# Padded heads of rounded k, single q buffers and a 24th resident weight tile in an attention and soft mixture-of-experts kernel

## The chip, the cores and the metric

The kernel runs on one core of a Trainium2 chip. It is one launch: causal attention over 96 heads, then a soft mixture of experts on the result. The metric is the device time of the launch in microseconds; smaller is better. Engine names are those of the profile: PE (TensorE, matmul), PEld (its weight loads), DVE (VectorE), ACT (ScalarE), POOL (GpSimd), SP (SyncE, which issues most DMAs).

## The reference

```python
# attention: batch 8, heads 12, seq 448, head_dim 64
scores = q @ k.T / 8, causal mask, softmax over keys      # per head
attn = softmax(scores) @ v
x = attn, transposed to (8 * 448, 768)
# soft mixture of experts: 8 experts of 4 slots, hidden 1024
logits = x @ phi                                          # (3584, 32)
d = softmax(logits, over tokens); c = softmax(logits, over slots)
slot_input = (d.T @ x) by expert                          # 8 x 4 x 768
slot_out = relu(slot_input @ w1[e]) @ w2[e]
out = c @ slot_out                                        # (3584, 768)
```

All is float32. q and k are drawn eight times larger than is usual, so the scores need the full precision.

## The kernel before

**Pairs and blocks.** Two heads make a pair; there are 48 pairs and 96 heads, head i = 2p + h. The function `block(p)` runs once per pair and works on several pairs at once: it finishes the scores of pair p, begins those of pair p + 1, prepares the operands of pairs p + 1 to p + 3, and multiplies the probabilities of pair p with v. Every engine executes its instructions in the order in which the program issues them (`_InOrder`); engines wait for each other through semaphores. So the text of `block` is the order of each queue.

**Scores in two passes.** The float32 matmul is replaced by matmuls with operands rounded to fp32r. The first pass (`scores1`) multiplies `ks` by `qd`. Rows 0 to 63 of `ks` hold the rounded k, rows 64 to 127 the remainder of k; `qd` holds the rounded q twice. The second pass (`scores2`) adds `k2` times `r2`: rows 64 to 127 are rounded k and the remainder of q, and the first rows carry the negative row maximum, block by block of 32 queries. In between, DVE reduces the first-pass scores to the maximum of each block of 32 queries (`max_keys`, `max_row`) and POOL spreads it into the first 14 rows of `r2` (`max_spread`, an affine_select). After the second pass ACT takes the exponential (`exps`).

**Preparing a pair.** The operands of a pair q come from HBM as raw q and raw k (`load_qk`). ACT rounds them (`cast_k` into `ks`, `cast_q` into `qd`), POOL computes the remainders in place (`sub_k` into rows 64 to 127 of `ks`, `sub_q` into rows 64 to 127 of `r2`), and ACT copies rounded k into `k2` (`copy_k2`). `ks`, `qd` and `r2` have two buffers, taken in turn by pairs; `k2` has one. The raw tiles rotate through a pool of four, so that a load waits for the subtraction that read the tile before.

**The order inside a block** (before), by engine, for a middle block p with heads a = 2p and a + 1:

- PE: second pass of head a, first pass of a + 2, second pass of a + 1, first pass of a + 3, probabilities times v for the pair, row maxima, parts of the experts' logits, four transposes.
- POOL: `sub_q(p+1)`, `sub_k(p+2)`, spread for head a + 2, spread for head a + 3. In block 4 it also clears `si`, the slot sums.
- ACT: exponential of head a, a copy of transposed x, exponential of a + 1, `copy_k2(p+1)`, `cast_q(p+2)`, `cast_k(p+3)`, and a few small operations of the logits in some blocks (`m6` = p modulo 6 tells which).
- SP: v of pair p + 1, in odd blocks one tile of expert weights, raw q of p + 3 (waits for `sub_q(p+1)`), raw k of p + 4 (waits for `sub_k(p+2)`).

```python
        if p:
            sub_q(p + 1)
            load_qk(p + 3, 0)
            sub_k(p + 2)
            load_qk(p + 4, 1)
        ...
        copy_k2(p + 1)
        ...
        cast_q(p + 2)
        cast_k(p + 3)
```

**Expert weights.** They are 64 tiles of 768 KB. `RES` = 23 tiles have places of their own from the start (eleven double tiles in `wres` and one single in `wone`) and are loaded in the odd blocks of attention. `TW1` = 12 more lie in a pool that opens when the buffers of attention are given back; each of its tiles lies over certain attention buffers and its load waits until those are free. SP issues them in order. All later tiles reuse places of tiles that the experts have consumed, so that their loads wait for PE. After them come the output's DMAs, 11 MB.

**The start.** Before block 0 the operands of pairs 0 and 1 are prepared by halves (one head at a time), and some matmuls on constants (`warm`, with counts in `START`) keep PE busy. Memsets on DVE and POOL clear padding and constants.

Of the kernel before, what the change touches and what calls it, by code (L numbers as in the profile page):

```python
# [9 lines left out]
F32 = mybir.dt.float32  # L10
# [3 lines left out]
ALU = mybir.AluOpType  # L14
# [18 lines left out]
NR, XB, XT = 2, 3, 2  # L33
RES, TW1 = 23, 12

HT = 2
WN, PAD = 1536, 168
WARM = (2, 5, 2, 3, 3)
START = (8, 3, 2)

# [40 lines left out]
def attention_soft_moe(ctx: ExitStack, tc: tile.TileContext, qk, va, phi, w1, w2, out):  # L81
    nc = _Core(tc)
    const = ctx.enter_context(tc.tile_pool(name="const", bufs=1, side="left"))
    wone = ctx.enter_context(tc.tile_pool(name="wone", bufs=1, side="left"))
    wres = ctx.enter_context(tc.tile_pool(name="wres", bufs=RES // 2, side="left"))
# [5 lines left out]
    fix = early.enter_context(tc.tile_pool(name="fix", bufs=1, side="right"))  # L91
    raw = early.enter_context(tc.tile_pool(name="raw", bufs=4, side="right"))
    ps_1 = att.enter_context(tc.tile_pool(name="ps_1", bufs=1, space=PSUM))
# [5 lines left out]
    x_, va_, pt_ = [None] * XB, [None, None], [None, None]  # L99
    qd_, ks_ = [fix.tile([P, 2, S], F32R, name="qd0")], [fix.tile([P, 2 * S + KP], F32R, name="ks0")]  # L100
    r2_ = [fix.tile([P, 2, S], F32R, name="r20")]
    qd_.append(fix.tile([P, 2, S], F32R, name="qd1"))
    ks_.append(fix.tile([P, 2 * S + KP], F32R, name="ks1"))
    va_[0] = fix.tile([P, NCH, 2, VC], F32, name="va0")
    x_[1] = fix.tile([P, NCH, 3 * P], F32, name="x1")
    r_ = [fix.tile([P, RW], F32, name=f"r{i}") for i in range(2)]
    k2_ = fix.tile([P, 2 * S + KP], F32R, name="k2")
    r2_.append(fix.tile([P, 2, S], F32R, name="r21"))
    pt_[0] = wk.tile([P, 1024], F32, name="pt0")
    va_[1] = wk.tile([P, NCH, 2, VC], F32, name="va1")  # L110
    pt_[1] = wk.tile([P, 1024], F32, name="pt1")
    ltn = moe.tile([P, P + 1], F32, name="lt")
    lt = ltn[:, 0:P]

    x_[2] = moe.tile([P, NCH, 3 * P], F32, name="x2")
    x_[0] = moe.tile([P, NCH, 3 * P], F32, name="x0")
    gs = moe.tile([P, P], F32, name="gs")
    mk = moe.tile([P, P], F32, name="mk")

    st = {}  # L120

    def load_qk(p, a, hs=slice(0, 2), eng=nc.sync):
        if p < NPAIR:
            if hs.start == 0:

                st["raw", a, p] = (wres.tile([P, 2 * WN], F32, tag="w", name=f"qk{a}_{p}")[:, 0:2 * S]
                                   .rearrange("p (h s) -> p h s", h=2)
                                   if (p, a) in ((1, 0), (2, 1)) else
                                   raw.tile([P, 2, S], F32, tag="qk", name=f"qk{a}_{p}"))
            eng.dma_start(out=st["raw", a, p][:, hs], in_=qk[p, :, a, hs])  # L130
# [20 lines left out]
    def slot(n, name, dtype=F32):  # L151
        m = place(n)
        if m >= RES:
            return wt[0].tile([P, WN], dtype, tag=f"wa{m}", name=name)
        if m == RES - 1:
            return wone.tile([P, WN], dtype, tag="w1", name=name)
        k = (n - m, m // 2)
        if k not in twos:
            twos[k] = wres.tile([P, 2 * WN], F32, tag="w", name=name)
        t = twos[k][:, WN * (m % 2):WN * (m % 2) + WN]  # L160
        return t if dtype is F32 else t.bitcast(dtype)

    def load_w(n):
        if n < len(order):
            m, e, h, u = order[n]
            t = wtiles[order[n]] = slot(n, f"w{n}")
            src, q = (w1 if m == 0 else w2)[e, h], place(n)
            if n <= NBUF or q >= RES - 1:
                nc.sync.dma_start(out=t, in_=src[:, WN * u:WN * u + WN])
            elif u:  # L170

                nc.sync.dma_start(out=twos[n - q, q // 2], in_=src)

    for hs in (slice(0, 1), slice(1, 2)):
# [20 lines left out]
    po0 = po2[:, 0:NCH]  # L195
    identb = const.tile([P, P], BF16, name="identb")

    for x in (x_[1], x_[0], x_[2]):
        nc.vector.memset(x[:, NCH - 1], 0.0)
    nc.scalar.activation(out=identb, in_=ident, func=AF.Copy)  # L200
    load_qk(1, 1, eng=nc.scalar)
    load_qk(2, 0)
    load_qk(3, 1)
    for i in range(NR):
        nc.gpsimd.memset(r2_[i][0:64, :, :].bitcast(F32), 0.0)
        nc.vector.memset(ks_[i][:, 2 * S:2 * S + KP].bitcast(F32), 0.0)
        nc.vector.memset(r_[i], -3.0e38)
    nc.vector.memset(k2_[0:64, 0:2 * S].bitcast(F32), 1.0)
    nc.vector.memset(k2_[:, 2 * S:2 * S + KP].bitcast(F32), 0.0)

# [12 lines left out]
    def kv(p):  # L223
        return ks_[p % NR][:, 0:2 * S].rearrange("p (h s)->p h s", h=2)

    def cast_q(p, hs=slice(0, 2)):
        if p < NPAIR:
            nc.scalar.activation(out=qd_[p % NR][:, hs], in_=st["raw", 0, p][:, hs], func=AF.Copy)

# [9 lines left out]
    def copy_k2(p, hs=slice(0, 2)):  # L239
        if p < NPAIR:  # L240
            nc.scalar.activation(out=k2_[64:P, 0:2 * S].rearrange("p (h s)->p h s", h=2)[:, hs], in_=kv(p)[0:64, hs],
                                 func=AF.Copy)

    def sub_q(p, hs=slice(0, 2), eng=None):
        if p < NPAIR:
            (eng or nc.gpsimd).tensor_tensor(out=r2_[p % NR][64:P, hs], in0=st["raw", 0, p][64:P, hs],
                                             in1=qd_[p % NR][64:P, hs], op=ALU.subtract)


    def scores1(i, part):  # L250
        if i >= NHD:
            return
        p, h = divmod(i, 2)
        ks, qd = ks_[p % NR], qd_[p % NR]
        if ("s", i) not in st:
# [7 lines left out]
        if part[0] == "k":  # L263
            c = int(part[1])
            o, w, m = S * h + P * c, S - CQ0[c], min(P, S - P * c + (KP if i > 4 or i % 2 else 0))
            nc.tensor.matmul(s[0:m, SCOL[c]:SCOL[c] + w], ks[:, o:o + m],
                             qd[:, h, CQ0[c]:S], start=start, stop=False, skip_group_check=True)
            return
# [46 lines left out]
    def max_spread(i):  # L315
        if i >= NHD:
            return
        p, h = divmod(i, 2)
        mr = st.pop(("mr", i))

        nc.gpsimd.affine_select(out=r2_[p % NR][0:NQB, h].rearrange("p (b t)->p b t", t=32),
                                in_=mr.unsqueeze(1).to_broadcast([NQB, NQB, 32]),
                                compare_op=ALU.is_equal, fill=0.0, base=0,
                                pattern=[[-1, NQB], [0, 32]], channel_multiplier=1)

    def scores2(i, cs):
        if i >= NHD:
            return
        p, h = divmod(i, 2)
        s = st["s", i]  # L330
        k2, r2 = k2_, r2_[p % NR]
        for c in cs:
            o, w, m = S * h + P * c, S - CQ0[c], min(P, S - P * c + (KP if i > 4 or i % 2 else 0))
            nc.tensor.matmul(s[0:m, SCOL[c]:SCOL[c] + w], k2[:, o:o + m],
                             r2[:, h, CQ0[c]:S], start=False, stop=True, skip_group_check=True)
# [152 lines left out]
    run_z = const.tile([P, 1], F32, name="run_z")  # L488
    si = const.tile([P, DM], F32, tag="si", name="si")
    lg = const.tile([P, NB, NCH, NSLOT], F32, name="lg")  # L490
# [477 lines left out]
```

## Time and profile before

| | |
|---|---|
| median of three runs | 404.35 us (403.54 to 404.68) |
| the profiled execution | 403.89 us, span 402.2 us |
| granted TensorE clock, mean | 0.984 |
| busy: PE, DVE, ACT, POOL | 368.3, 293.7, 282.4, 265.3 us |
| DMA moved | 119.17 MB, mean 296 GB/s |

The span is the time from the first to the last instruction. All instructions carry the same source line (a helper's, L65), so the rows are told apart by engine, operation and tiles. In a timeline row the columns are the start, the duration, engine, line, operation, written tile and read tiles, shapes and count; in brackets stands the idle time of the engine before it and what ended it. On PE, `s<-qd,ks` is the first pass and `s<-r,k` the second. On POOL, `r<-qk,qd` is `sub_q`, `ks<-qk,ks` is `sub_k`, and the affine select `r<-mr` is a spread. On ACT, `qd<-qk` is `cast_q`, `ks<-qk` is `cast_k`, `k<-ks` is `copy_k2`, `pt<-s` the exponential. On SP, `w<-in_w_dram` are expert weights. The name `r` stands for `r2`, for the maxima and for a few more, since numbers are left out of names.

### The profile page before, as it was taken

How to read it: one execution, taken by the hardware profiler on the slowest of the kernel's cores; microseconds unless marked ns; L12 is line 12 of the kernel's file. 1: busy time of each engine (PE TensorE's matmuls, PEld its weight loads, DVE VectorE, ACT ScalarE, POOL GpSimd, SP SyncE). 2: the span in 40 equal slices, each digit the busy share in tenths (PEclk: the TensorE clock that was granted, in tenths of full speed). 3: DMA queues.
4: the chain of work that ended last, by engine and by line, in shares of the span. 5: the costliest groups of instructions: out<-in, count | busy, mean ns of one | idle time of the engine just before them, and what ended most of it. 6: DMA issues, size and time to landing. Idle time of an engine off the chain costs nothing.

```text
span 402.2 us, 14066 instructions
## 1 busy us (share of the span) xinstructions
PE 368.3 (92%) x5756; PEld 295.8 (74%) x5756; DVE 293.7 (73%) x834; ACT 282.4 (70%) x395; POOL 265.3 (66%) x214
## 2 busy tenths in 40 slices
PE   6889899999999999999999999999999989997840
PEld 3678888898988898888888889888876544542420
DVE  5868788788898888898888888888975575342540
ACT  5878798898898888888888988988952112432430
POOL 5899899898898988898988989888950000000000
PEclk9999999999999999999999999999999999999985
DMA  8668877878787788777788787788679999999997
GB/s 304 230 199 282 271 266 228 245 279 278 229 286 262 244 269 289 256 240 265 262 270 259 249 272 238 274 286 257 216 279 415 420 420 423 424 418 413 398 397 339
DMA packets 34480, 119.17 MB, mean 296 GB/s; under 512 B 3824, under 2 KB 8944, under 8 KB 32880
## 3 DMA queue, kind: packets, MB, share of 16 engines
q1 hardware_dynamic: 34128, 117.55, 82.2%
q8 instruction: 45, 0.74, 0.7%
q10 hardware_dynamic: 288, 0.73, 0.5%
q14 instruction: 19, 0.16, 0.1%
HBM read 107.25 MB, written 11.01 MB: 294 GB/s over the span
## 4 chain that ended last, share of the span: by engine, by line
PE 54%; DMA 16%; POOL 12%; issue 5%; ACT 4%; DVE 4%; SPq 1%; POOLq 0%; DVEq 0%; ACTq 0%
PE s L65 28%; PE po L65 17%; DMA w<-in_w_dram 14%; POOL r L65 7%; POOL ks L65 5%; PE xm L65 3%; PE rt L65 1%; ACT ks L65 1%; PE pp L65 1%; DVE r L65 1%; DMA qk<-in_qk_dram 1%; PE hp L65 1%; ACT k L65 1%; DVE si L65 1%; PE e L65 1%
## 5 line engine op out<-in xcount | busy, mean ns | idle before, releaser
L65 DVE TRANSPOSE_TENSOR_REDUCE r<-s 128x32 f32<-128x1024 f32 x96 | 119.5, 1245 | 11.4 <-PE s L65 9.3
L65 ACT ACTIVATE pt<-s 128x1024 f32<-128x1024 f32 x96 | 98.8, 1029 | 40.6 <-PE s L65 37.8
L65 PEld LDWEIGHTS po<-va,pt 128*64 128x64 f32 x3040 | 103.6, 138 | 12.0 <-issue 11.9
L65 PE MATMUL po<-va,pt 128*64 128x65 f32 x3040 | 110.6, 224 | 0.0
L65 POOL TENSOR_TENSOR r<-qk,qd 64x896 fp32r<-64x896 f32 (+1 forms) x50 | 101.7, 2033 | 5.5 <-ACT qd L65 1.8
L65 POOL TENSOR_TENSOR ks<-qk,ks 64x896 fp32r<-64x896 f32 (+1 forms) x49 | 99.2, 2024 | 0.2
L65 PE MATMUL s<-qd,ks 128*128 128x448 f32 (+4 forms) x384 | 80.8, 322 | 0.6 <-POOL ks L65 0.4
L65 POOL TENSOR_SCALAR_AFFINE_SELECT r<-mr 14x448 fp32r<-14x448 f32 x96 | 61.5, 643 | 29.8 <-PE xm L65 18.6
L65 PE MATMUL s<-r,k 128*128 128x448 f32 (+3 forms) x384 | 65.2, 292 | 5.0 <-POOL r L65 4.3
L65 PEld LDWEIGHTS s<-r,k 128*128 128x128 f32 (+1 forms) x384 | 59.3, 176 | 11.0 <-POOL r L65 8.8
L65 PEld LDWEIGHTS s<-qd,ks 128*128 128x128 f32 (+2 forms) x384 | 52.8, 184 | 3.7 <-issue 1.4
L65 ACT ACTIVATE qd<-qk 128x896 fp32r<-128x896 f32 (+1 forms) x50 | 46.0, 920 | 1.7 <-DMA qk<-in_qk_dram 0.8
L65 ACT ACTIVATE k<-ks 64x896 fp32r<-64x896 f32 (+1 forms) x49 | 45.8, 934 | 1.2
L65 ACT ACTIVATE ks<-qk 128x896 fp32r<-128x896 f32 (+1 forms) x51 | 45.4, 892 | 1.1 <-DMA qk<-in_qk_dram 1.0
L65 PE MATMUL s<-tri,identb 128*128 128x192 bf16 x192 | 39.4, 270 | 1.1 <-DVE si L65 0.4
L65 DVE TENSOR_REDUCE r<-r 128x16 f32<-128x32 f32 x192 | 33.7, 176 | 5.0
L65 DVE TENSOR_REDUCE mr<-s 14x32 f32<-14x128 f32 x47 | 13.1, 279 | 23.1 <-ACT ks L65 12.8
L65 PE MATMUL xm<-ident,x 128*128 128x128 f32 x188 | 28.3, 273 | 0.0
L65 ACT ACTIVATE xts<-xm 128x512 f32<-128x512 f32 x47 | 27.8, 592 | 0.2 <-PE xm L65 0.2
L65 DVE TENSOR_SCALAR x<-po,sm 64x64 f32<-64x64 f32 x94 | 25.9, 276 | 0.7
L65 DVE TENSOR_TENSOR x<-po,sm 128x384 f32<-128x384 f32 (+2 forms) x49 | 25.7, 526 | 0.0
L65 DVE COPY ot<-pp 128x384 f32<-128x384 f32 x26 | 13.6, 554 | 13.4 <-PE pp L65 13.3
(138 smaller groups left out, 391.0 us busy)
## 6 DMA issues: line engine op xcount, KB each, us to landing
qk<-in_qk_dram SPq DMA_DIRECT2D x93, 448.0 KB, 4.4
w<-in_w_dram SPq DMA_DIRECT2D x43, 768.0 KB, 7.0
w<-in_w_dram SPq DMA_DIRECT2D x10, 1536.0 KB, 21.0
va<-in_va_dram SPq DMA_DIRECT2D x47, 260.0 KB, 4.6
out_dram<-ot SPq DMA_DIRECT2D x16, 384.0 KB, 6.7
out_dram<-ot SPq DMA_DIRECT2D x2, 1536.0 KB, 9.2
qk<-in_qk_dram SPq DMA_DIRECT2D x4, 224.0 KB, 3.9
hw<-in_w_dram SPq DMA_DIRECT2D x1, 768.0 KB, 8.4
```

Source lines behind the costliest of these rows:

```text
L65: return self._tc.keep_in_program_order(op(*args, **kwargs))
```

## The change

- Two zero columns stand behind each head of `ks` and `k2` (row of 2 x 450 instead of 2 x 448 + 2), so that the last chunk of either head reads zeros and not its neighbour. Operations on k now address two runs of 448.
- `qd` and `r2` have one buffer each. In a middle block POOL does `sub_k(p+2)` first, then `sub_q(p+1)`; ACT does `cast_k(p+3)` first, then `cast_q(p+2)`; the loads follow. Blocks 0 and 1 have an order of their own by halves.
- The raw tiles are two fixed ones for k and two for q, and the order of buffers in memory changes.
- `RES` = 24 and `TW1` = 11: twelve double tiles are resident, `wone` is gone, and blocks 16 and 30 load a weight tile as well as the odd blocks up to 43.
- `si` is cleared by DVE before all pairs and no longer by POOL in block 4.
- At the start, k of pair 1 is loaded through SP's queue and no longer through ACT's; the warm-up counts change from (8, 3, 2) to (9, 6, 2, 4).

```diff
+KS = S + KP
-RES, TW1 = 23, 12
+RES, TW1 = 24, 11
-START = (8, 3, 2)
+START = (9, 6, 2, 4)
...
-    wone = ctx.enter_context(tc.tile_pool(name="wone", bufs=1, side="left"))
-    raw = early.enter_context(tc.tile_pool(name="raw", bufs=4, side="right"))
...
+    kraw = {n: fix.tile([P, 2, S], F32, name=f"kraw{n}") for n in (0, 1)}
+    qraw = {0: fix.tile([P, 2, S], F32, name="qraw0")}
+    ks_ = [fix.tile([P, 2 * KS], F32R, name="ks0")]
+    qd = fix.tile([P, 2, S], F32R, name="qd")
+    ks_.append(fix.tile([P, 2 * KS], F32R, name="ks1"))
+    qraw[1] = fix.tile([P, 2, S], F32, name="qraw1")
     va_[0] = fix.tile([P, NCH, 2, VC], F32, name="va0")
+    r_ = [fix.tile([P, RW], F32, name=f"r{i}") for i in range(2)]
     x_[1] = fix.tile([P, NCH, 3 * P], F32, name="x1")
-    k2_ = fix.tile([P, 2 * S + KP], F32R, name="k2")
-    r2_.append(fix.tile([P, 2, S], F32R, name="r21"))
+    k2_ = fix.tile([P, 2 * KS], F32R, name="k2")
+    r2 = fix.tile([P, 2, S], F32R, name="r2")
...
     for hs in (slice(0, 1), slice(1, 2)):
         load_qk(0, 1, hs)
         load_qk(0, 0, hs)
+    load_qk(1, 1)
     load_qk(1, 0)
...
-    load_qk(1, 1, eng=nc.scalar)
     load_qk(2, 0)
-    load_qk(3, 1)
...
+    nc.vector.memset(si, 0.0)
...
-            o, w, m = S * h + P * c, S - CQ0[c], min(P, S - P * c + (KP if i > 4 or i % 2 else 0))
+            o, w, m = KS * h + P * c, S - CQ0[c], min(P, KS - P * c)
...
     sub_k(0, h1)
+    load_qk(3, 1)
     max_row(0, 0)
...
-        if p % 2 and p // 2 < RES - 1 or p == 2 * RES - 2:
-            load_w(p // 2)
+        if p % 2 and p < 44 or p in (16, 30):
+            load_w(st["w"])
+            st["w"] += 1
...
         if p == 0:
             copy_k2(0, h1)
             cast_q(1, h1)
+            warm(START[3], pob)
             max_row(1, 0)
...
-        elif p == 4:
-            nc.gpsimd.memset(si, 0.0)
...
-        if p:
+        late_k = p == 1
+        if p == 1:
+            sub_q(2, h0)
+            sub_k(3, h0)
+            sub_q(2, h1)
+            load_qk(4, 0)
+        elif p:
+            sub_k(p + 2, h0 if late_k else slice(0, 2))
+            if not late_k:
+                load_qk(p + 4, 1)
             sub_q(p + 1)
             load_qk(p + 3, 0)
-            sub_k(p + 2)
-            load_qk(p + 4, 1)
         else:
             sub_q(1, h0)
+            sub_q(1, h1)
+            load_qk(3, 0)
             sub_k(2, h0)
         copy_k2(p + 1)
...
-        cast_q(p + 2)
-        cast_k(p + 3)
+        if p:
+            cast_k(p + 3)
+            cast_q(p + 2)
+        else:
+            cast_q(2)
+            cast_k(3)
...
         max_spread(a + 2)
         if p == 0:
-            sub_q(1, h1)
-            load_qk(3, 0)
+            sub_k(2, h1)
+            load_qk(4, 1)
...
         max_spread(a + 3)
-        if p == 0:
-            sub_k(2, h1)
-            load_qk(4, 1)
+        if late_k:
+            sub_k(p + 2, h1)
+            load_qk(p + 4, 1)
```

More of the change, by code (lines that the diff above doesn't have):

```diff
@@ L99, in attention_soft_moe, with heads @@
     x_, va_, pt_ = [None] * XB, [None, None], [None, None]
[L100 to L103, printed above, removed]
+    kraw = {n: fix.tile([P, 2, S], F32, name=f"kraw{n}") for n in (0, 1)}
[4 more added lines that the diff above has]
+    qraw[1] = fix.tile([P, 2, S], F32, name="qraw1")
     va_[0] = fix.tile([P, NCH, 2, VC], F32, name="va0")
+    r_ = [fix.tile([P, RW], F32, name=f"r{i}") for i in range(2)]
     x_[1] = fix.tile([P, NCH, 3 * P], F32, name="x1")
-    r_ = [fix.tile([P, RW], F32, name=f"r{i}") for i in range(2)]
-    k2_ = fix.tile([P, 2 * S + KP], F32R, name="k2")
-    r2_.append(fix.tile([P, 2, S], F32R, name="r21"))
+    k2_ = fix.tile([P, 2 * KS], F32R, name="k2")
+    r2 = fix.tile([P, 2, S], F32R, name="r2")
     pt_[0] = wk.tile([P, 1024], F32, name="pt0")
+    pt_[1] = wk.tile([P, 1024], F32, name="pt1")
     va_[1] = wk.tile([P, NCH, 2, VC], F32, name="va1")
-    pt_[1] = wk.tile([P, 1024], F32, name="pt1")
+    x_[2] = moe.tile([P, NCH, 3 * P], F32, name="x2")
+    x_[0] = moe.tile([P, NCH, 3 * P], F32, name="x0")
     ltn = moe.tile([P, P + 1], F32, name="lt")
     lt = ltn[:, 0:P]
-    x_[2] = moe.tile([P, NCH, 3 * P], F32, name="x2")
-    x_[0] = moe.tile([P, NCH, 3 * P], F32, name="x0")
     gs = moe.tile([P, P], F32, name="gs")
     mk = moe.tile([P, P], F32, name="mk")
-    st = {}
+    st = {"w": 0}
+    def heads(t):
+        return t.rearrange("p (h s) -> p h s", h=2)
     def load_qk(p, a, hs=slice(0, 2), eng=nc.sync):
@@ L128, in load_qk @@
                                    if (p, a) in ((1, 0), (2, 1)) else
-                                   raw.tile([P, 2, S], F32, tag="qk", name=f"qk{a}_{p}"))
+                                   kraw[p % 2 if p > 1 else 1 - p] if a else qraw[p % 2 if p else 1])
             eng.dma_start(out=st["raw", a, p][:, hs], in_=qk[p, :, a, hs])
@@ L154, in slot @@
             return wt[0].tile([P, WN], dtype, tag=f"wa{m}", name=name)
-        if m == RES - 1:
-            return wone.tile([P, WN], dtype, tag="w1", name=name)
         k = (n - m, m // 2)
@@ L167, in load_w @@
             src, q = (w1 if m == 0 else w2)[e, h], place(n)
-            if n <= NBUF or q >= RES - 1:
+            if n <= NBUF or q >= RES:
                 nc.sync.dma_start(out=t, in_=src[:, WN * u:WN * u + WN])
@@ L196, in attention_soft_moe @@
     identb = const.tile([P, P], BF16, name="identb")
+    si = const.tile([P, DM], F32, tag="si", name="si")
     for x in (x_[1], x_[0], x_[2]):
@@ L200, in attention_soft_moe @@
     nc.scalar.activation(out=identb, in_=ident, func=AF.Copy)
-    load_qk(1, 1, eng=nc.scalar)
     load_qk(2, 0)
-    load_qk(3, 1)
+    nc.gpsimd.memset(r2[0:64, :, :].bitcast(F32), 0.0)
     for i in range(NR):
-        nc.gpsimd.memset(r2_[i][0:64, :, :].bitcast(F32), 0.0)
-        nc.vector.memset(ks_[i][:, 2 * S:2 * S + KP].bitcast(F32), 0.0)
+        nc.vector.memset(heads(ks_[i])[:, :, S:KS].bitcast(F32), 0.0)
         nc.vector.memset(r_[i], -3.0e38)
-    nc.vector.memset(k2_[0:64, 0:2 * S].bitcast(F32), 1.0)
-    nc.vector.memset(k2_[:, 2 * S:2 * S + KP].bitcast(F32), 0.0)
+    nc.vector.memset(k2_[0:64, :].bitcast(F32), 1.0)
+    nc.vector.memset(heads(k2_)[:, :, S:KS].bitcast(F32), 0.0)
+    nc.vector.memset(si, 0.0)
     def misc(name):
@@ L223, in kv @@
     def kv(p):
-        return ks_[p % NR][:, 0:2 * S].rearrange("p (h s)->p h s", h=2)
+        return heads(ks_[p % NR])[:, :, 0:S]
     def cast_q(p, hs=slice(0, 2)):
         if p < NPAIR:
-            nc.scalar.activation(out=qd_[p % NR][:, hs], in_=st["raw", 0, p][:, hs], func=AF.Copy)
+            nc.scalar.activation(out=qd[:, hs], in_=st["raw", 0, p][:, hs], func=AF.Copy)
     def cast_k(p, hs=slice(0, 2)):
@@ L240, in copy_k2 @@
         if p < NPAIR:
-            nc.scalar.activation(out=k2_[64:P, 0:2 * S].rearrange("p (h s)->p h s", h=2)[:, hs], in_=kv(p)[0:64, hs],
+            nc.scalar.activation(out=heads(k2_)[64:P, hs, 0:S], in_=kv(p)[0:64, hs],
                                  func=AF.Copy)
@@ L245, in sub_q @@
         if p < NPAIR:
-            (eng or nc.gpsimd).tensor_tensor(out=r2_[p % NR][64:P, hs], in0=st["raw", 0, p][64:P, hs],
-                                             in1=qd_[p % NR][64:P, hs], op=ALU.subtract)
+            (eng or nc.gpsimd).tensor_tensor(out=r2[64:P, hs], in0=st["raw", 0, p][64:P, hs],
+                                             in1=qd[64:P, hs], op=ALU.subtract)
     def scores1(i, part):
@@ L253, in scores1 @@
         p, h = divmod(i, 2)
-        ks, qd = ks_[p % NR], qd_[p % NR]
+        ks = ks_[p % NR]
         if ("s", i) not in st:
@@ L319, in max_spread @@
         mr = st.pop(("mr", i))
-        nc.gpsimd.affine_select(out=r2_[p % NR][0:NQB, h].rearrange("p (b t)->p b t", t=32),
+        nc.gpsimd.affine_select(out=r2[0:NQB, h].rearrange("p (b t)->p b t", t=32),
                                 in_=mr.unsqueeze(1).to_broadcast([NQB, NQB, 32]),
@@ L330, in scores2 @@
         s = st["s", i]
-        k2, r2 = k2_, r2_[p % NR]
+        k2 = k2_
         for c in cs:
-            o, w, m = S * h + P * c, S - CQ0[c], min(P, S - P * c + (KP if i > 4 or i % 2 else 0))
+            o, w, m = KS * h + P * c, S - CQ0[c], min(P, KS - P * c)
             nc.tensor.matmul(s[0:m, SCOL[c]:SCOL[c] + w], k2[:, o:o + m],
@@ L488, in attention_soft_moe @@
     run_z = const.tile([P, 1], F32, name="run_z")
-    si = const.tile([P, DM], F32, tag="si", name="si")
     lg = const.tile([P, NB, NCH, NSLOT], F32, name="lg")
```

## The prediction

> **What bounds the kernel now.** I read the page first (busy shares, the slices, the chain), then windows of the closing part, then the timeline of single blocks by engine.
>
> ```profile
> span 402.2 us, 14066 instructions
> PE 368.3 (92%) x5756; PEld 295.8 (74%) x5756; DVE 293.7 (73%) x834; ACT 282.4 (70%) x395; POOL 265.3 (66%) x214
> POOL 5899899898898988898988989888950000000000
> DMA  8668877878787788777788787788679999999997
> PE 54%; DMA 16%; POOL 12%; issue 5%; ACT 4%; DVE 4%; SPq 1%; POOLq 0%; DVEq 0%; ACTq 0%
> ```
>
> There are two kernels in one span. For thirty of the forty slices (attention) POOL is busy eight or nine tenths and DMA has room; in the last ten POOL is silent and DMA is full. The chain names PE and POOL for the first part and DMA for the second. So each edit has to be priced in the part where it falls. The closing part, by windows (stretch; length; busy of PE, PEld, DVE, ACT, POOL; clock; DMA share; GB/s):
>
> ```profile
> 288.00:292.00 4.00, 4.00 (x100) 3.62 (x98) 3.53 (x9) 3.77 (x6) 3.93 (x3) 1.00 0.05 16
> 292.00:298.00 6.00, 5.99 (x107) 5.33 (x103) 5.00 (x14) 3.86 (x6) 3.03 (x4) 1.00 0.73 221
> 298.00:312.00 14.00, 12.70 (x199) 8.99 (x189) 7.76 (x31) 4.71 (x11) 2.28 (x9) 1.00 1.01 412
> 312.00:374.50 62.50, 56.27 (x701) 28.45 (x700) 30.01 (x93) 16.04 (x43) 0.00 (x0) 1.00 1.01 419
> 396.00:400.00 4.00, 0.00 (x0) 0.00 (x0) 0.00 (x0) 0.00 (x0) 0.00 (x0) 0.50 0.94 399
> ```
>
> From 298 to nearly 400 the DMA engines never rest, at 399 to 419 GB/s. The end is therefore bytes over rate, and only fewer bytes, or bytes moved earlier, change it. From 288 to 298 the engines had spare time.
>
> The attention part, for two blocks that I use below (38, then 39 from 250.03; 36 and 37):
>
> ```profile
> 245.10 2.11 POOL L65 TENSOR_TENSOR r<-qk,qd 64x896 fp32r<-64x896 f32 x1
> 247.16 2.10 POOL L65 TENSOR_TENSOR ks<-qk,ks 64x896 fp32r<-64x896 f32 x1
> 249.34 1.27 POOL L65 TENSOR_SCALAR_AFFINE_SELECT r<-mr 14x448 fp32r<-14x448 f32 x2
> 248.68 0.94 ACT L65 ACTIVATE qd<-qk 128x896 fp32r<-128x896 f32 x1
> 249.52 0.94 ACT L65 ACTIVATE ks<-qk 128x896 fp32r<-128x896 f32 x1
> 250.03 0.73 PE L65 MATMUL s<-r,k 128*128 128x448 f32 x4
> 250.65 0.25 PE L65 MATMUL s<-qd,ks 128*66 128x64 f32 x1
> 251.32 0.63 PE L65 MATMUL s<-r,k 128*128 128x448 f32 x4
> 234.92 2.09 POOL L65 TENSOR_TENSOR ks<-qk,ks 64x896 fp32r<-64x896 f32 x1
> 238.78 0.25 PE L65 MATMUL s<-qd,ks 128*66 128x64 f32 x1
> ```
>
> Block 38 is limited by POOL: sub_q, sub_k and two spreads stand without a gap, and the second-pass scores of block 39 begin (250.03) as the first of the two spreads ends. Other blocks leave POOL a wait, and PE paces them.
>
> **The change, part by part.**
>
> *q's remainder in one buffer (r2).* sub_q(p+1) writes rows that the second-pass scores of pair p still read, so on POOL it gains a wait for PE. The new order puts sub_k(p+2) ahead of it, the same 2.10 us. In block 39 sub_k would run from the end of the spreads, 249.34 + 1.27 = 250.6, to 252.7, and the scores it waits for end at 251.32 + 0.63 = 251.95: 0.8 us of cover. POOL does the same work in the same time, and both spreads keep their place behind it. Price 0. If sub_k were gone the wait would cost what is left of it; that happens in block 46, which has no sub_k (48), and where the spread behind it waits 1.97 us for DVE anyway:
>
> ```profile
> 293.66 2.11 POOL L65 TENSOR_TENSOR r<-qk,qd 64x896 fp32r<-64x896 f32 x1
> 297.73 0.64 POOL L65 TENSOR_SCALAR_AFFINE_SELECT r<-mr 14x448 fp32r<-14x448 f32 x1 [1.97 <-DVE mr L65]
> ```
>
> *Rounded q in one buffer (qd), and cast_k ahead of cast_q.* cast_q(p+2) on ACT now waits for sub_q(p+1), which ends where sub_k ended before. Block 36: 234.92 + 2.09 = 237.01, cast 0.95, done by 238.0, with the first-pass scores that need it at 238.78: 0.7 us to spare. Block 38 is the tightest: sub_q ends at 249.26; cast_k takes the first place (248.68 to 249.6), cast_q the second, done at 250.46 where cast_k ended before; the scores start at 250.65. Margin 0.19 us. Queued behind cast_q on ACT is the exponential of the next block, which needs PE's scores of 250.03 + 0.73 = 250.76 first. Price 0; bounds 0 and 0.2 us in one block of six, some 1.5 us.
>
> *Loads.* SP now issues k(p+4) at the end of sub_k and q(p+3) at the end of sub_q: each about 2.1 us earlier or later than before, with the next v and w behind them at the old time. The cast that needs q comes some 6 us after the issue.
>
> ```profile
> qk<-in_qk_dram SPq DMA_DIRECT2D x93, 448.0 KB, 4.4
> ```
>
> Landing takes 4.4 us in the median, so 0. The two extra loads of w (blocks 16, 30) and the one that moves go into slices at 6 to 8 tenths: 0.
>
> *Zero columns behind each head.* Matmul shapes stay (66 columns of k were already read in the last chunk). Casts, copies and subtractions of k now write two runs of 448 instead of one of 896. Lower bound 0; upper bound, the price of two half instructions:
>
> ```profile
> L65 POOL TENSOR_TENSOR ks<-qk,ks 64x896 fp32r<-64x896 f32 x45 | 94.6, 2103 | 0.0
> L65 POOL TENSOR_TENSOR ks<-qk,ks 64x448 fp32r<-64x448 f32 x4 | 4.6, 1138 | 0.2
> L65 ACT ACTIVATE k<-ks 64x896 fp32r<-64x896 f32 x47 | 44.6, 950 | 1.2
> L65 ACT ACTIVATE k<-ks 64x448 fp32r<-64x448 f32 x2 | 1.2, 577 | 0.0
> L65 ACT ACTIVATE c<-lg 128x256 fp32r<-128x256 f32 x8 | 2.7, 404 | 6.1 <-PE so L65 4.6 <-PE hp L65 1.4
> ```
>
> Two halves cost 2 x 1138 - 2103 = 173 ns more on POOL and 2 x 577 - 950 = 204 ns more on ACT. But the ACT rows give 0.83 ns an element over a fixed 204 ns, hence an estimate of 417 ns for 256 elements in one run, and the last row wrote 256 in runs of 32 in 404 ns. Runs are free there; I take 0 on both engines.
>
> *Slot sums cleared ahead of all pairs.* The memset leaves POOL in block 4, where it is on the path:
>
> ```profile
> 37.48 0.73 POOL L65 MEMSET si<- 128x768 f32 x1
> 38.30 2.10 POOL L65 TENSOR_TENSOR r<-qk,qd 64x896 fp32r<-64x896 f32 x1
> 42.53 1.24 POOL L65 TENSOR_SCALAR_AFFINE_SELECT r<-mr 14x448 fp32r<-14x448 f32 x2
> 43.22 0.47 PE L65 MATMUL s<-r,k 128*128 128x448 f32 x1 [1.03 <-POOL r L65]
> ```
>
> PE waits 1.03 us for the spread behind it, so the full 0.73 us can go: -0.7 (bounds -0.73 and 0). On DVE the new memset falls into the start, and its price is in the bounds of the next part.
>
> *The start.* k(1) moves from ACT's queue into SP's, so q(0) does not share the engines with it; its cast waits for it now:
>
> ```profile
> 4.75 0.58 ACT L65 ACTIVATE qd<-qk 128x448 fp32r<-128x448 f32 x1 [0.75 <-DMA qk<-in_qk_dram]
> 5.37 0.32 PE L65 MATMUL s<-qd,ks 128*64 128x64 f32 x1 [0.23 <-ACT qd L65]
> 11.48 0.28 PE L65 MATMUL rt<-ident,r 128*76 128x128 f32 x1 [0.68 <-DVE r L65]
> 12.31 0.60 PE L65 MATMUL po<-tri,identb 128*128 128x512 bf16 x2
> 19.08 1.14 POOL L65 TENSOR_TENSOR ks<-qk,ks 64x448 fp32r<-64x448 f32 x1
> 25.09 0.47 PE L65 MATMUL s<-r,k 128*128 128x448 f32 x1 [1.08 <-POOL r L65]
> ```
>
> A ninth warm-up matmul stands between, so I expect little of that back: scores at 5.1 to 5.4 instead of 5.37. Four more warm-ups in block 0 take 2 x 0.60 us by the row of the two others, ahead of a row maximum where PE stood idle for 0.68: 0.5 us late at most. In block 1 the reordering lets the spread for block 2 start after three half subtractions (3 x 1.14) instead of 1.14 + 2 x 2.09, 1.9 us earlier; PE can use the 1.08 us that it waited there. POOL then owes the postponed half and catches up only in block 3, and the load of k(5), issued a half later, may hold cast_k(5) and the cast_q(4) behind it. Net -0.1, bounds -1.2 and +1.0.
>
> *The 24th resident tile.* One 768 KB load leaves the full stretch for the loose one. And more moves with it: the closing loads are issued as the buffers beneath them fall free. Before, the first was issued at 291.33 (sub_k(47)), the second at 295.79 (sub_q(47)):
>
> ```profile
> 291.33 7.98 SPq L65 DMA_DIRECT2D w<-in_w_dram  x6
> 301.11 10.18 SPq L65 DMA_DIRECT2D w<-in_w_dram  x6
> ```
>
> Laying the listed buffers out by size gives all twelve issue times of before. The same sum after: first tile under the two k buffers, free after sub_k(47), now first on POOL in block 45, at 289.2; second after sub_q(46), 291.3; third after sub_q(47), which now waits for PE's scores as above, about 297; the last as before (the sixth at 301.1, two near 311). A tile takes 786 KB / 0.419 = 1.88 us. Of 41 tiles still to load, 221 GB/s x 6 us = 1.33 MB, at most 1.7 tiles, had been moved by 298, and 39.3 or more were left; after, 2 of 40 are moved and 38 are left. That is 1.3 tiles or 2.4 us, and 3.1 us if a third of a tile of those bytes was the last v. The last two closing loads, issued near 311 as x falls free, meet a queue that is then nearly empty and may cost 0.2. So -2.5, bounds -3.1 and -0.5 (queue empty for 2 us).
>
> [...]
>
> *Sum.* -0.7 - 0.1 - 2.5 = -3.3 us. The profiled execution took 403.89 us (span 402.2), inside the runs (403.54 to 404.68, median 404.35), 0.46 below their median. The sum gives 400.6 against itself and 401.05 against the median; I say 400.8.
>
> **The rivals.**
>
> *Two runs cost like two instructions.* 204 ns twice on ACT and 173 ns on POOL per block. Only block 38's kind has no room (margin 0.19 on ACT, none on POOL): some 0.4 us in each of seven, 2.8 us, giving 403.5. Against it: the 404 ns row.
>
> *The closing queue runs dry.* Loads 7 to 11 wait for buffers until 304 to 311, and with one tile less ahead of them the engines idle. The term falls to -0.5, giving 402.6. For it: a few tenths of margin; against it: before, the share stayed at 1.01 through that stretch, with about two tiles in hand at its end.
>
> *Slower: single buffers make a ring.* Scores, sub_q, cast_q, scores again become one loop through PE, POOL and ACT. Its own length is 2.11 + 0.95 + 0.67 + 0.63, about 4.5 us with hand-overs, under the 6.07 us of a block (sub_q at 293.66 less 245.10, over eight). But POOL's place for sub_q is second, and PE sees every tenth beyond the 0.19 to 0.7 us margins: 0.1 us a block is 4.6 us and already turns the sign; 0.2 us is 9.2 us and gives 410. [...] By the rows above each wait is covered.
>
> *Slower: closing tiles fall on late buffers.* If the new order of buffers put the first closing tile on k2 (free at 301.1), every load queues behind it: 40 tiles from about 302 instead of 39.3 from 298, 4 + 1.3 = +5.3, less 0.8, giving 408. Against it is that the layout sum met all twelve times.
>
> **How the numbers follow.** Forecast 0.63 (its own range 398.9 to 402.3); two runs 0.10; dry queue 0.12; ring 0.10; late buffers 0.05. What a measurement can tell from no change is 0.3%, 1.2 us: 403.1 to 405.6. Faster takes the forecast but 0.01, most of the dry queue and a third of the first rival: 0.75. Same gets 0.11, slower 0.14. The low end is all lower bounds together (-0.73 - 1.2 - 3.1 = -5.0 from 403.9: 398.9); the high end takes in the dry queue and the two runs and stops at 404.0, leaving out the slower cases.
>
> **What would show it.** Right: blocks still 6.07 us apart in the middle; no ACT wait on POOL over 0.2 us before cast_q and no PE wait on qd; the second-pass scores of block 5 near 42.4; one w less issued after attention, the first near 288.5; DMA full from 298 on; the last weights about 3 us earlier. Wrong: k casts or copies near 1.15 us, POOL waiting on PE ahead of sub_q in the middle, or DMA idle between 300 and 312.

## The result, and the profile after

| | before | after |
|---|---|---|
| median, side by side | 404.89 us (403.54 to 406.25) | 399.65 us (399.07 to 399.94) |
| ratio | | 0.9868 (95%: 0.9844 to 0.9892) |
| the profiled execution | 403.89 us, span 402.2 | 399.68 us, span 398.0 |

The kernel became 1.3% faster. One execution of the kernel after ran at a granted clock of 0.559 and took 582.88 us; it is left out of the range and of the ratio, and without it the median is 399.62. The head of the page and its chain, kernel after:

```profile
span 398.0 us, 14037 instructions
PE 368.5 (93%) x5764; PEld 296.6 (75%) x5764; DVE 294.6 (74%) x835; ACT 283.2 (71%) x395; POOL 256.6 (64%) x214
...
POOL 5998889888898888898898898888950000000000
...
DMA  7868887777997778877988877788579999999997
...
PE 68%; DMA 12%; POOL 8%; ACT 3%; DVE 3%; issue 2%; POOLq 0%; DVEq 0%; ACTq 0%; SPq 0%
```

POOL's busy time fell from 265.3 to 256.6 us, although only two memsets (0.73 and about 0.8 us) left it, and its share of the chain fell from 12% to 8%. PE, ACT and DVE are as busy as before.

Where the time went is read from one marker per block: the first row of the second pass, `s<-r,k`, on PE. The marker of the last block, 47, in the kernel before:

```profile
299.35 0.71 PE L65 MATMUL s<-r,k 128*128 128x448 f32 x4
```

The kernel after, timeline of PE, with the markers of blocks 5, 39, 40 and 47:

```profile
41.59 0.73 PE L66 MATMUL s<-r,k 128*128 128x448 f32 x4 [0.18 <-POOL r L66]
...
246.44 0.74 PE L66 MATMUL s<-r,k 128*128 128x448 f32 x4
...
252.60 0.60 PE L66 MATMUL s<-r,k 128*128 128x448 f32 x2
...
295.61 0.72 PE L66 MATMUL s<-r,k 128*128 128x448 f32 x4
```

Block 47 begins at 295.61, 3.74 us earlier; the span is 4.2 us shorter. In this pair of profiles attention gave 3.74 us and the closing part 0.46. I had forecast 0.8 and 2.5. The total was right and its two halves were not: that the two errors cancelled was luck.

The kernel after, groups by form, the operations on k and q:

```profile
L66 POOL TENSOR_TENSOR r<-qraw,qd 64x896 fp32r<-64x896 f32 x45 | 94.7, 2104 | 1.3 <-ACT pt L66 1.3
...
L66 POOL TENSOR_TENSOR ks<-kraw,ks 64x896 fp32r<-64x896 f32 x44 | 85.5, 1944 | 3.4
...
L66 ACT ACTIVATE qd<-qraw 128x896 fp32r<-128x896 f32 x46 | 43.5, 945 | 0.9 <-POOL r L66 0.7 <-DMA qraw<-in_qk_dram 0.2
...
L66 ACT ACTIVATE k<-ks 64x896 fp32r<-64x896 f32 x47 | 44.7, 951 | 1.2
```

`sub_k` takes 1944 ns where it took 2103; experiment 2 shows which part of its new layout made it faster. `sub_q` is as it was. The last columns answer the question of single buffers: over all full-size operations POOL waited 1.3 us ahead of `sub_q` and ACT 0.7 us for POOL ahead of `cast_q`. Each is a single wait, the first in block 46, which has no `sub_k` left (the prediction had named it), the second in block 45, which has no `cast_k` left.

The kernel after, windows (stretch; length; busy of PE, PEld, DVE, ACT, POOL; clock; DMA share; GB/s):

```profile
298.00:302.00 4.00, 3.47 (x79) 2.99 (x79) 1.79 (x10) 1.44 (x2) 0.19 (x1) 1.00 1.04 410
302.00:306.00 4.00, 3.79 (x49) 2.23 (x53) 2.00 (x9) 1.41 (x5) 0.00 (x0) 1.00 0.96 301
306.00:312.00 6.00, 6.00 (x100) 4.03 (x95) 2.23 (x10) 0.56 (x3) 0.00 (x0) 1.00 1.01 401
312.00:370.00 58.00, 52.29 (x646) 26.28 (x638) 29.37 (x90) 15.76 (x42) 0.00 (x0) 1.00 1.01 420
```

Before, the rate was 412 GB/s over all of 298 to 312. Now it drops to 301 for 4 us. The DMA share hardly shows it (0.96), the GB/s do. This looks like the rival "the closing queue runs dry", but by the issues and landings in the trace three or four loads were on their way all through these 4 us, and four or five at the same place of the kernel before. The queue was thinner but not empty.

### The profile page after: what moved, and what is told of

The parts are those of the page before. It is cut to its first block, busy times and chain, and to the rows that moved or that the text cites. A ratio compares the mean times of both kernels' runs of the same rounds, so it can differ in the third digit from the quotient of the medians.

```text
span 398.0 us, 14037 instructions
## 1 busy us (share of the span) xinstructions
PE 368.5 (93%) x5764; PEld 296.6 (75%) x5764; DVE 294.6 (74%) x835; ACT 283.2 (71%) x395; POOL 256.6 (64%) x214
## 4 chain that ended last, share of the span: by engine, by line
PE 68%; DMA 12%; POOL 8%; ACT 3%; DVE 3%; issue 2%; POOLq 0%; DVEq 0%; ACTq 0%; SPq 0%
PE s L66 34%; PE po L66 21%; DMA w<-in_w_dram 12%; POOL r L66 6%; PE xm L66 4%; POOL ks L66 3%; PE hp L66 3%; PE rt L66 2%; PE pp L66 1%; ACT qd L66 1%; PE warm L66 1%; PE so L66 1%; PE e L66 1%; DVE si L66 1%; ACT ot L66 1%
## 5 line engine op out<-in xcount | busy, mean ns | idle before, releaser
L66 POOL TENSOR_TENSOR r<-qraw,qd 64x896 fp32r<-64x896 f32 (+1 forms) x49 | 99.3, 2026 | 3.2 <-ACT qd L66 1.8
L66 POOL TENSOR_TENSOR ks<-kraw,ks 64x896 fp32r<-64x896 f32 (+1 forms) x48 | 89.7, 1870 | 4.2 <-ACT ks L66 0.6
L66 PE MATMUL s<-qd,ks 128*66 128x64 f32 (+3 forms) x384 | 80.7, 321 | 0.0
L66 PEld LDWEIGHTS s<-qd,ks 128*128 128x128 f32 (+1 forms) x384 | 52.7, 183 | 2.1 <-issue 0.8
L66 ACT ACTIVATE ks<-kraw 128x896 fp32r<-128x896 f32 (+1 forms) x49 | 45.0, 920 | 4.7 <-DMA kraw<-in_qk_dram 3.5
L66 ACT ACTIVATE qd<-qraw 128x896 fp32r<-128x896 f32 (+1 forms) x48 | 44.6, 930 | 2.1 <-DMA qraw<-in_qk_dram 1.4
```

Source lines behind the costliest of these rows:

```text
L66: return self._tc.keep_in_program_order(op(*args, **kwargs))
```

## The experiments

Beside medians I use two distances in each profile: from the marker of block 0 (or 3, behind the start) to that of block 47, and from there to the end of the span. The marker of block 0 itself lies anywhere from 9.2 to 10.1 us, so the distance is the safer number. The experiments ran in several sessions, in which the median of the kernel before lay between 404.3 and 405.5 us; differences of about 1 us between medians are therefore better read from the ratios.

**1. The 24th tile taken back.**

```diff
-RES, TW1 = 24, 11
+RES, TW1 = 23, 12          # and wone, the single place, again
-        if p % 2 and p < 44 or p in (16, 30):
+        if p % 2 and p < 44 or p == 44:
```

> The changed kernel with 23 resident weight tiles and 12 closing ones again (one load in block 44 in place of those in blocks 16 and 30); all else as changed. Theory A (the closing queue runs dry, so the tile is worth little): 0.5 us longer than the changed kernel, about 400.2 us, with attention ending at the same time (second pass of the last block near 295.6 us) and DMA full and at over 395 GB/s in every 2 us from 298 to 312. Theory B (the forecast's term holds and the attention part gave less than the trace says): 2.5 us longer, about 402.2 us.

Measured: 399.2 us, ratio 0.9865 (0.9841 to 0.9889), the same as with 24 tiles. The rate dips here too, by windows of this run:

```profile
298.00:302.00 4.00, 3.37 (x73) 2.86 (x71) 2.02 (x11) 0.93 (x3) 0.00 (x0) 1.00 1.11 404
302.00:306.00 4.00, 3.88 (x63) 2.38 (x66) 2.01 (x8) 1.27 (x5) 0.00 (x0) 1.00 0.88 292
306.00:312.00 6.00, 6.00 (x95) 3.95 (x91) 2.37 (x11) 0.69 (x3) 0.00 (x0) 1.00 1.02 409
```

B fell, and A's full queue with it. With the new order of buffers the additional closing load is the first to be issued, at 282.2, still in the loose stretch, so the tile saves no bytes of the full stretch: by the trace 40.8 MB were still to move at the marker of block 47, with 23 tiles as with 24. What limits both is probably when buffers come free, by the waits of SP listed further down; no run shows that by itself.

**2. Heads of k aligned again.** In the kernel after a head takes 450 words, so head 1 starts at byte 1800 of the row, 8 past the place where head 1 of raw k starts (1792). Here it takes 452; the matmuls read the same columns.

```diff
-KS = S + KP
+KS = S + 2 * KP
```

> The changed kernel with heads of k 452 apart and not 450, so that head 1 begins at a multiple of 16 bytes as head 0 does. Theory A (sub_k is faster because head 1 begins 8 bytes past such a multiple): sub_k back from 1.94 to 2.10 us, the blocks after p = 6n + 2 5.95 us long and not 5.78, the time 1.0 to 1.5 us longer, about 400.9 us. Theory B (two runs are quicker than one, wherever they lie): sub_k stays at 1.94 us and the time at 399.7 us.

Measured: 401.45 us, ratio 0.9921 (0.9896 to 0.9945), 1.8 us over the kernel after. Groups by form:

```profile
L66 POOL TENSOR_TENSOR ks<-kraw,ks 64x896 fp32r<-64x896 f32 x44 | 92.9, 2112 | 3.4
```

Two runs cost 9 ns more than one on POOL; the 8 bytes were what saved 159 ns. The halves at the start of the kernel after show the same inside one profile, head 1 of pair 2 and then head 0 of pair 3:

```profile
17.29 0.98 POOL L66 TENSOR_TENSOR ks<-qk,ks 64x448 fp32r<-64x448 f32 x1
20.17 1.15 POOL L66 TENSOR_TENSOR ks<-kraw,ks 64x448 fp32r<-64x448 f32 x1
```

The distance from block 3 to 47 is 267.22 us against 265.74 after: 1.48 us, all in the blocks that POOL paces.

**3. `sub_q` ahead of `sub_k`, with one buffer for q's remainder** (the old order on POOL).

```diff
-            sub_k(p + 2, h0 if late_k else slice(0, 2))
-            if not late_k:
-                load_qk(p + 4, 1)
             sub_q(p + 1)
             load_qk(p + 3, 0)
+            sub_k(p + 2)
+            load_qk(p + 4, 1)
```

> The changed kernel with sub_q(p+1) ahead of sub_k(p+2) on POOL again, with the single buffers. Theory A (sub_k is what covers sub_q's wait for PE's second pass): POOL waits about 1.0 us for PE ahead of each sub_q, a block grows from 6.07 to about 6.7 us and the time by some 25 to 30 us, to about 427 us. Theory B (the wait is short or lies beside PE's work anyway): within 1 us of 399.7 us.

Measured: 433.62 us, ratio 1.0719 (1.0674 to 1.0764). Timeline of POOL in this run:

```profile
243.34 2.10 POOL L66 TENSOR_TENSOR r<-qraw,qd 64x896 fp32r<-64x896 f32 x1 [1.51 <-ACT pt L66]
245.41 1.94 POOL L66 TENSOR_TENSOR ks<-kraw,ks 64x896 fp32r<-64x896 f32 x1
247.41 1.24 POOL L66 TENSOR_SCALAR_AFFINE_SELECT r<-mr 14x448 fp32r<-14x448 f32 x2
250.17 2.11 POOL L66 TENSOR_TENSOR r<-qraw,qd 64x896 fp32r<-64x896 f32 x1 [1.51 <-ACT pt L66]
```

1.51 us of waiting in each block, and blocks 6.83 us long. The profile names ACT; what `sub_q` must wait for by the program is the second pass, whose rows it overwrites. On PE that pass ends at 242.57 + 0.63 = 243.20, and `sub_q` begins at 243.34:

```profile
242.57 0.63 PE L66 MATMUL s<-r,k 128*128 128x448 f32 x4
```

So the single buffer is free only because `sub_k` stands ahead of it: this is the ring that I had as a rival.

**4. Both inputs that POOL subtracts moved 8 bytes.** `ks` and `qd` start 8 bytes into their tiles; the raw tiles stay.

```diff
-    ks_ = [fix.tile([P, 2 * KS], F32R, name="ks0")]
-    qd = fix.tile([P, 2, S], F32R, name="qd")
+    ks_ = [fix.tile([P, 2 * KS + 2], F32R, name="ks0")[:, 2:2 * KS + 2]]
+    qd = fix.tile([P, 2 * S + 2], F32R, name="qd")[:, 2:2 * S + 2].rearrange("p (h s) -> p h s", h=2)
...
+KS = S + 2 * KP
```

> The changed kernel with rounded k and rounded q each shifted so that both heads begin 8 bytes past a multiple of 16 bytes (two unused columns ahead, heads of k 452 apart). Theory A (the place of the second input against the first sets POOL's rate): sub_k 1.78 us, sub_q 1.94 us; POOL-bound blocks shorten until PE binds (5.78 to about 5.6 us), 1 to 2 us in all, about 398.2 us. Theory B (it is the place of the output): sub_q stays at 2.10 us, gain 0.5 us or less. Theory C (shifted operands slow PE or ACT): slower than 399.7 us.

Measured: 397.7 us, ratio 0.9834 (0.9809 to 0.986): the fastest kernel here. It is 2 us under the kernel after by the medians and 1.4 by the ratios, whose intervals overlap; from block 0 to 47 it takes 283.92 us against 285.80. Groups by form:

```profile
L66 POOL TENSOR_TENSOR r<-qraw,qd 64x896 fp32r<-64x896 f32 x45 | 79.8, 1773 | 1.3 <-ACT pt L66 1.3
L66 POOL TENSOR_TENSOR ks<-kraw,ks 64x896 fp32r<-64x896 f32 x44 | 77.9, 1770 | 3.4
```

I had expected 1.94 for `sub_q`; it went to 1.77, since here both heads are shifted and in the kernel after only head 1. In block 38 POOL now waits 0.22 and 0.51 us for DVE ahead of its two spreads, so a faster POOL would bring little more there.

**5. A second profile of the kernel before**, unchanged.

> The kernel before, profiled a second time. In its first profile the blocks 10, 31 and 32 were 0.36, 0.09 and 0.39 us longer than their like. Theory A (chance): from the second pass of block 3 to that of block 47 it takes about 267.9 us and not 268.7, so that 0.8 us of the attention part's gain of 3.7 us is the first profile's own. Theory B (the kernel's own): the same blocks are long again and it takes 268.7 us.

Measured: 404.51 us; block 3 to 47 took 268.66 us, against 268.69. A block is counted here from its marker to the next. Three blocks of before were longer than their kind, 4 (6.63 us), 10 (6.42) and 32 (6.33). They are so again (6.63, 6.44, 6.31): A fell.

**6. The slot sums cleared on POOL in block 4 again.**

```diff
-    nc.vector.memset(si, 0.0)
...
+        elif p == 4:
+            nc.gpsimd.memset(si, 0.0)
```

> The changed kernel with the slot sums cleared by POOL in block 4 again. Theory A (the memset was on the path): block 5 begins 0.7 us later against block 4 (6.5 us after it and not 5.77), the time 0.7 us longer, about 400.4 us. Theory B (PE paces that block now, since sub_k is faster): 399.7 us.

Measured: 400.17 us, ratio 0.9883 (0.986 to 0.9905). Timelines of POOL and of PE in this run:

```profile
36.81 0.73 POOL L66 MEMSET si<- 128x768 f32 x1
...
41.68 1.24 POOL L66 TENSOR_SCALAR_AFFINE_SELECT r<-mr 14x448 fp32r<-14x448 f32 x2
```

```profile
42.38 0.73 PE L66 MATMUL s<-r,k 128*128 128x448 f32 x4 [0.86 <-POOL r L66]
```

Block 4 takes 6.45 us, against 5.77: 0.68 us, as forecast. But blocks 10 (6.43 against 6.06) and 32 (6.14 against 5.78) are long again too, some 0.36 us each: of the three long blocks of before, these two had not been in my sum. In block 10 the maximum reduction of DVE stands idle for 1.09 us, until PE's transposes end, and begins 0.31 us behind the block's marker; in the kernel after it waits 0.73 and begins 0.05 us ahead of it. First this run, then the kernel after:

```profile
72.29 0.28 DVE L66 TENSOR_REDUCE mr<-s 14x32 f32<-14x128 f32 x1 [1.09 <-PE xm L66]
```

```profile
71.15 0.28 DVE L66 TENSOR_REDUCE mr<-s 14x32 f32<-14x128 f32 x1 [0.73 <-ACT qd L66]
```

Why the reduction then waits for the later transposes, and why just in these blocks, is not settled. That the memset's place brings it is shown, since nothing else differs; the profiles of the kernel before, of experiment 5 and of experiment 8, all with the memset in block 4, show the same late start (about 0.31 us) in blocks 10 and 32. From block 3 to 47 it is worth 267.06 - 265.74 = 1.32 us; the timed difference is smaller, 0.6 us by the ratios, and their intervals overlap.

**7. `cast_q` ahead of `cast_k`, with one buffer for rounded q.**

```diff
-            cast_k(p + 3)
             cast_q(p + 2)
+            cast_k(p + 3)
```

> The changed kernel with cast_q(p+2) ahead of cast_k(p+3) on ACT again, with the single buffer of rounded q. Theory A (cast_q's wait for sub_q costs nothing only because cast_k stands ahead of it): ACT waits 0.3 to 0.9 us for POOL in every block, cast_k ends that much later, and the exponential and sub_k behind it are late by 0.1 to 0.4 us in some blocks: 2 to 8 us longer, about 404 us. Theory B (the rounded k has a block of time, the exponential too): 399.7 us.

Measured: 404.19 us, ratio 0.9969 (0.9951 to 0.9987): most of the gain is gone. Groups by form:

```profile
L66 ACT ACTIVATE qd<-qraw 128x896 fp32r<-128x896 f32 x46 | 43.8, 953 | 33.4 <-POOL r L66 33.4
```

ACT waits 33.4 us for `sub_q`, against 0.7. Most of it is slack; from block 9 on the path pays 0.17 us in blocks 6n + 3 and 0.52 in blocks 6n + 4. Block 0 to 47 takes 290.58 us, 4.8 more.

**8. The kernel before, with nothing but the 8 bytes.** Its `ks` and `qd` (two buffers each) shifted as in 4.

```diff
-    qd_, ks_ = [fix.tile([P, 2, S], F32R, name="qd0")], [fix.tile([P, 2 * S + KP], F32R, name="ks0")]
+    qd_, ks_ = [fix.tile([P, 2 * S + 2], F32R, name="qd0")[:, 2:2 * S + 2].rearrange("p (h s) -> p h s", h=2)], [fix.tile([P, 2 * S + KP + 2], F32R, name="ks0")[:, 2:2 * S + KP + 2]]
```

> The kernel before with its two buffers of rounded k and of rounded q each shifted by two columns (8 bytes); nothing of the change. Theory A (POOL's rate by the place of its second input, not by the change's other parts): sub_k and sub_q near 1.77 us, the POOL-bound blocks 5.6 us long and not 5.95, the time 2 to 3 us shorter than before, about 402 us. Theory B (the rate needs the two runs or the new places of the raw tiles): 2.10 us and 404.3 us.

Measured: 400.67 us, ratio 0.9894 (0.9868 to 0.9921). Groups by form:

```profile
L65 POOL TENSOR_TENSOR r<-qk,qd 64x896 fp32r<-64x896 f32 x46 | 81.4, 1769 | 3.6
L65 POOL TENSOR_TENSOR ks<-qk,ks 64x896 fp32r<-64x896 f32 x45 | 79.8, 1774 | 0.0
L65 POOL TENSOR_TENSOR r<-qk,qd 64x448 fp32r<-64x448 f32 x4 | 3.9, 976 | 2.0 <-ACT qd L65 1.8
```

Addresses alone give the old kernel 1.1%, nearly as much as the whole change gave. They do more here than in the change: both heads of `ks` and `qd` are shifted, where the change shifted one head of `ks`.

**9 and 10. Which address counts.** In 9 the raw q and the rounded q are both shifted by 8 bytes; in 10 only the output of `sub_q`.

```diff
9: -    qraw = {0: fix.tile([P, 2, S], F32, name="qraw0")}
9: +    qraw = {0: fix.tile([P, 2 * S + 2], F32, name="qraw0")[:, 2:2 * S + 2].rearrange("p (h s) -> p h s", h=2)}
9: ...   # qraw1 and qd in the same way
10: -    r2 = fix.tile([P, 2, S], F32R, name="r2")
10: +    r2 = fix.tile([P, 2 * S + 2], F32R, name="r2")[:, 2:2 * S + 2].rearrange("p (h s) -> p h s", h=2)
```

> The kernel after, with the two inputs of sub_q, the raw q and the rounded q, both placed 8 bytes past a multiple of 16; its output and everything of k stay as in the kernel after. Theory A, what counts is where the two inputs stand to each other: sub_q goes back to, or stays at, 2.10 us, and the POOL-paced blocks stay at 5.78 us. Theory B, what counts is that any operand starts off a multiple of 16: sub_q takes 1.77 us, as it did with the rounded q alone shifted, and those blocks take about 5.6 us.

> The kernel after, with only the output of sub_q (q's remainder) placed 8 bytes past a multiple of 16. Theory A, only the two inputs count: sub_q 2.10 us. Theory B, any operand counts: sub_q about 1.8 us and the POOL-paced blocks about 5.6 us.

Measured: single executions of 398.25 and 398.54 us; block 3 to 47 took 265.69 and 265.77 us, as after (265.74). Groups by form, 9 and then 10:

```profile
L66 POOL TENSOR_TENSOR r<-qraw,qd 64x896 fp32r<-64x896 f32 x45 | 94.6, 2103 | 1.3 <-ACT pt L66 1.3
```

```profile
L66 POOL TENSOR_TENSOR r<-qraw,qd 64x896 fp32r<-64x896 f32 x45 | 94.7, 2103 | 1.3 <-ACT pt L66 1.3
```

In neither is `sub_q` faster. Theory A holds, B falls: what counted in these runs is where the two inputs stand to each other (1773 ns in experiment 4, with one of them shifted; 2103 with both), not that one is shifted, and not the output (2103).

**11. The old warm-ups.**

```diff
-START = (9, 6, 2, 4)
+START = (8, 3, 2, 0)
```

> The kernel after with the warm-up matmuls of the kernel before: eight, three and two instead of nine, six and two, and none of the four new ones in block 0. Theory A, the new warm-ups cost up to half a us and hide nothing: the second-pass scores of blocks 0 to 2 begin 0.3 to 0.6 us earlier and the time is 0.3 to 0.6 us under the kernel after. Theory B, they stand in waits: within 0.3 us of the kernel after. Theory C, they hold the clock up: a granted clock under 1.00 in the first 15 us, and a time over that of the kernel after by half a us or more.

Measured: 399.04 us, ratio 0.9848 (0.981 to 0.9886). That overlaps the kernel after (0.9868). From block 0 to 3 it takes 20.04 us against 20.07, with a mean granted clock over the span of 0.983 and 0.984. B: the extra matmuls stand in waits.

## Why the prediction came out right, point by point

**Single buffers (0): right.** At the head of block 39 `sub_k` runs from 247.26 to 249.21 and the second pass that it covers ends at 248.37, 0.84 us of cover where I had worked out 0.8. Experiments 3 and 7 show what the two covers are worth: 34 us and 4.5 us (4.1 by the ratios). The forecast priced the waits from their cover, and the cover was there. In the order of the kernel after, the two single buffers left one wait each, 1.3 us on POOL and 0.7 us on ACT. Kernel after, POOL and then PE:

```profile
247.26 1.95 POOL L66 TENSOR_TENSOR ks<-kraw,ks 64x896 fp32r<-64x896 f32 x1
249.16 2.11 POOL L66 TENSOR_TENSOR r<-qraw,qd 64x896 fp32r<-64x896 f32 x1
```

```profile
247.74 0.63 PE L66 MATMUL s<-r,k 128*128 128x448 f32 x4
```

**Zero columns (0, bounds 0 and 2.8): wrong, and the step that failed.** "Runs are free there; I take 0 on both engines" holds for runs: ACT's copy takes 951 ns (950 before), POOL's aligned subtraction 2112 (2103). But the step looked only at the number of runs and not at where the second one starts, and its lower bound was 0 with no reason that excluded a gain. The subtraction lost 159 ns, and in the blocks that POOL paces all of it came off the path: block 38 fell from 5.95 to 5.78 us. Experiment 2 prices it at 1.48 us from block 3 on and 1.8 us in the time.

**Slot sums (-0.7): right in place, short in size.** Block 4 gave 0.68 us (experiment 6). The markers of before could have told the rest: blocks 10 and 32 were 0.36 and 0.38 us longer than their kind, and I had not asked why. All three went, 1.3 us in the profile.

These two explain attention. From block 3 to 47: 268.69 before, 265.74 after, -2.95; 1.48 + 1.32 = 2.80 is accounted for. I had -0.7 for the same stretch.

**The start (-0.1, bounds -1.2 and +1.0): inside its bounds.** Block 0 to 3 went from 20.59 to 20.07 us; with the heads aligned it is 20.82. That would give the faster `sub_k` about 0.7 and the reordering and the warm-ups nothing. But the same distance is 20.05, 20.45 and 20.28 us in the profiles of experiments 1, 6 and 10, which leave blocks 0 to 3 as they are, so some 0.4 us of this may be scatter and the split is not settled.

**The 24th tile (-2.5, bounds -3.1 and -0.5): mis-sized.** From the last marker to the end of the span: 102.85, 103.92 and 103.46 us in three profiles with the old order of buffers (before, experiments 5 and 8), 101.31 to 102.39 in nine with the new order and 24 tiles (after, experiments 2 to 4, 6, 7 and 9 to 11), mean 102.0. The means differ by 1.4 us; the pair of the forecast differs by only 0.46.

The bytes of the sum were right. By the trace 41.8 MB were still to move at the last marker in the three profiles with the old order, and 40.8 MB in all with the new: 1.0 MB, the 1.3 tiles of the forecast, 2.4 us at 0.42 MB a us. The issue times were right too: first closing load forecast at 289.2, measured 285.5 in a kernel that ends attention 3.7 us earlier. The sum went wrong where it took the stretch as full and put only "0.2" on the last two loads. The windows of after lack 4 x (412 - 301) + 6 x (412 - 401) = 510 us x GB/s, 1.2 us at 420 GB/s, and at 302 to 306 this comes ahead of those two. That is in effect the rival "the closing queue runs dry", for which I had named the loads that wait for buffers until 304 to 311. The 412 is not a fixed mark: in experiment 5, the kernel before again, the 14 us at the same place moved 388, with the fall around the marker of block 47 and not 6 us behind it. Over the first 16 us behind the marker the kernels with the new order lack 1.1 to 1.6 us of the 420 rate, the three profiles with the old order 0.2 to 1.0. What SP waited for then, kernel after, from 285 to 312 (total, times, longest):

```profile
SPq L66 <- ACT k L66: 6.2, 2, 5.2
SPq L66 <- PE e L66: 3.6, 4, 2.1
SPq L66 <- PE s L66: 2.9, 2, 1.6
SPq L66 <- POOL ks L66: 2.6, 1, 2.6
```

Before, a backlog of four or five loads bridged these waits; now three or four stand there, with 23 tiles as with 24, so it was not the tile that thinned the queue; the new order of buffers is the likely reason. Why three or four loads on their way move only 301 GB/s is not settled: in experiment 10, with the same order, the same 4 us, counted from the marker, moved 390, and its closing part took 101.44 us. The tile itself is worth nothing that the times can tell (experiment 1; by the single profile with 23 tiles, 102.82 us against a mean of 102.0, up to 0.8). Which part of the 1.4 us belongs to the order of buffers alone I did not try.

So 399.65 against a forecast of 400.8 is a right total from two wrong terms, by luck: from block 0 to 47 attention gave 2.7 us more than the sum had, and the closing part 1 to 2 us less. Of the signs that the prediction named, the blocks in the middle (6.03 us apart, 6.07 forecast) and the closing load that went were right; block 5 began at 41.59 and not near 42.4, and "DMA full from 298 on" was not.

## What to carry to other kernels

Price a change of layout by the new start addresses as well as by the number of runs (here 8 bytes took 159 ns off a subtraction, and two runs added 9), and leave the gain side open where no row excludes it. When blocks of one kind differ in length in the profile, ask for the reason before pricing anything: two blocks that were nearly 0.4 us too long stood there unexplained, and the edit removed both. When bytes leave a full DMA stretch, ask whether the stretch stays full: here 2.4 us of bytes left it and about 1.4 us arrived, and the rate fell to 301 GB/s for 4 us while the loads behind them waited for buffers.

## What the runs showed of the hardware

A POOL subtraction of two float32 inputs, 64 x 896, took 2103 and 2111 ns in the kernel before, where neither input is shifted, and 1770 and 1773 in experiment 4 (1774 and 1769 in experiment 8), where one is shifted by 8 bytes; `sub_k` took 1944 in the kernel after, where only head 1 of rounded k is. With both inputs shifted by 8 bytes (experiment 9) or the output alone (experiment 10), `sub_q` took 2103. In experiment 2 head 1 of rounded k stands 16 bytes off that of raw k, and `sub_k` took 2112. No other distances were tried, and no other operation. The kernel before, groups by form:

```profile
L65 POOL TENSOR_TENSOR r<-qk,qd 64x896 fp32r<-64x896 f32 x46 | 97.1, 2111 | 3.6
L65 POOL TENSOR_TENSOR r<-qk,qd 64x448 fp32r<-64x448 f32 x4 | 4.6, 1144 | 1.9 <-ACT qd L65 1.8
```

From these and the same rows of experiment 8, an estimate for one element in each of the 64 rows is (2111 - 1144) / 448 = 2.16 ns without the shift and (1769 - 976) / 448 = 1.77 with it.
